# A fused retention and feed-forward kernel: the second projection of six blocks as seven products of quarters, in a new order of the work

## The chip, the core and the metric

The kernel runs on one core of a Trainium2 chip. The core has a matrix engine (TensorE, PE in the profile, with its weight loads as PEld), a vector engine (DVE), a scalar engine (ACT), a general engine (POOL, GpSimd) and a queue engine that here only issues transfers (SP). They run side by side, each through its own list of instructions in order, and wait for each other by semaphores. Data moves between HBM and on-chip memory by 16 DMA engines, which SP, ACT and POOL feed. TensorE adds its results up in eight banks of 512 f32 columns by 128 partitions; DVE and ACT read the banks, POOL cannot.

The metric is the time of one execution in microseconds on the device, lower is better.

## The reference

```python
def _attn_ref(q, k, v):                      # each (8, 8, 576, 64): batch, heads, rows, width
    scores = scale * np.matmul(q, k.transpose(0, 1, 3, 2))
    ...
    Dmat = np.where(rel >= 0, gamma[:, None, None] ** rel[None, :, :], 0.0)
    ret = scores * Dmat[None, :, :, :]
    return np.matmul(ret, v).astype(np.float32)

def _moe_ref(x, w_in, w_out, alpha):         # x: 4608 tokens of 512; w_in 512x2048, w_out 2048x512
    h = x @ w_in
    s = np.sin(alpha * h)
    g = h + s * s / (alpha + 1e-09)
    return (g @ w_out).astype(np.float32)
```

The heads' outputs of the first part, side by side, are the 512 columns of `x` in the second. Everything comes and goes as f32; the matrix engine works on f16 copies.

## The kernel before

**Blocks.** The 4608 tokens are nine blocks of 512. Blocks 0 to 7 are the first 512 rows of the eight batches; block 8 is made of the last 64 rows of all of them. For each block the kernel computes the retention and then the feed-forward part:

- LD loads q, k or v of one half of a block (256 rows of all heads, 512 KB) into one of sixteen f32 buffers; CA scales and casts it to f16. LE and CE do the same for the last 64 rows.
- k and q are turned by TensorE and a copy (TU, TK) in blocks 0 and 1, and by a transposing transfer (XP, XE) after that.
- OU, TS or EV, MA, MB, NS and ST build the states that carry the decayed past from one 128 rows to the next. SC makes the scores in a pair of banks, MK masks them out of the banks on DVE, VA, VB and SA add up values and states in a pair of banks (RL is a mark between the two), KP copies the result to `x`.
- PR is a first projection of 128 hidden units: four matmuls of 512 tokens into one bank. SI takes the sine of the bank (ACT), SQ squares it (ACT, DVE or POOL), and PD, on DVE, adds the scaled square to the bank's contents and writes `g`; only then is the bank free. There are 16 units to a block.
- G2 is a quarter of a second projection: four matmuls of 128 tokens x 512 columns, sixteen (four G2) to a bank for 128 tokens. FI copies the bank out, OS sends it to the output in two transfers.

WI and WO are the eight transfers of the weights, issued by POOL, which cast from f32 to f16 on the way. G2.n.c.p reads the rows of `w_out` that WO.p brings. KB are matmuls on zeros that fill waits of TensorE early on.

**The order** is not found at run time: it is the list `STEPS` (line 23 on). Each step has the form `kind.numbers:engine name=place`, where the engine letter is A (ACT), V (DVE), G (POOL) or P (PE); PD, MK, NS and AD are always on DVE, SI on ACT. `name=place` puts a tile into a numbered buffer or bank, and `<step` makes a step wait for another. The loop at line 896 emits the steps one by one, so every engine runs its steps in the order of the list. All waits that data, buffers and banks need are set by the framework; a step waits for them with everything behind it on its engine.

In `PR.1.7.2 hps.1.7=6`, for instance, unit 7 of block 1 goes into bank 6, with all 512 tokens (the last 2; 0 and 1 are the halves of 256). A score, value or `o` name takes two banks: `o.1.0=0` is banks 0 and 1.

Around the place where the two orders part, the kernel before does the following. SP issues its loads without a pause as buffers allow: all six of block 0, then 1.q.1, 1.q.0, 1.v.0, 1.k.0, 1.k.1, 1.v.1, 2.k.1, 2.k.0, 2.q.0, 2.v.0, 2.v.1, 3.k.1. POOL issues WI.0, WI.2, WI.1, WI.3, WO.0, WO.1, WO.2, WO.3. TensorE, at the end of block 0's first projection, runs PR.0.15, PR.0.13, G2.0.1.0, G2.0.1.1, SC.1.0.1, OU.1.0, SC.1.0.0, G2.0.3.0, G2.0.3.1, TU.1.k.1.2, G2.0.3.2, SC.1.1.1, SC.1.1.0, OU.1.1, G2.0.1.2, G2.0.0.0, the values and states of block 1, G2.0.3.3, G2.0.1.3, and then block 1's first projection. DVE runs there PD.0.13, the two halves of TK.1.k.1, MK.1.1.1, MK.1.1.0, ST.1.2, NS.1.3, and only then casts of block 2: CA.2.k.1.0, CA.2.k.1.1, CA.2.k.0.2. From block 3 on, units of one block's first projection alternate with the second projection of the block before, one PR to one G2.

The functions TT, SM, PP, CP, AD and OQ stand in the file but no step before calls them.

Of the kernel before, what the change touches and what calls it, by code (L numbers as in the profile page):

```python
# [23 lines left out]
CN; AR; EY; MC; Z0; ZE; FS; LD.0.k.0 raw.0.k.0=0; LD.0.q.0 raw.0.q.0=1; LD.0.v.0 raw.0.v.0=2; LD.0.q.1 raw.0.q.1=3  # L24
LD.0.k.1 raw.0.k.1=4; CA.0.k.0.0:G k16.0.0=0; LD.0.v.1 raw.0.v.1=5; CA.0.q.0.1:V q16.0.0=1; CA.0.k.0.1:V; CA.0.q.0.0:V
CA.0.v.0.2:A v16.0.0=2; LD.1.q.1 raw.1.q.1=6; KB.16.256.6; KB.44.64.6; OU.0.0 kv.0.0.0=0 kv.0.0.1=1
# [188 lines left out]
def kernel(  # L215
# [10 lines left out]
    nc = tc.nc  # L226
# [4 lines left out]
    P = 128  # L231
# [77 lines left out]
    def halves(n):  # L309
        return slice(64 * n, 64 * n + 64)  # L310
# [631 lines left out]
```

## Time and profile before

| | |
|---|---|
| median of three runs | 311.0 us (309.82 to 311.75) |
| profiled execution | 310.68 us |
| its span, first to last instruction | 308.9 us |
| granted TensorE clock, mean | 0.991 |
| first projection (L757), 608 matmuls | 143.1 us busy |
| second projection (L796), 576 matmuls | 142.3 us busy |
| DMA packets | 49.84 MB, 161 GB/s on average |

Line numbers are those of the listing above: L757 is PR, L765 SI, L775 and L776 SQ, L780 PD, L796 G2, L313 all copies and casts, L436 CA of q and k, L386 WO, L539 SC, L570 VA and VB, L606 SA, L552 MK, L512 MA, L515 MB, L520 NS, L526 ST. "L780 DVE ... x144 | 106.2, 746 | 54.3 <-ACT s L775 46.1" means: 144 instructions of that line on DVE were busy for 106.2 us, 746 ns each; before them DVE sat idle for 54.3 us, 46.1 of which ended with ACT's instruction of line 775. In a timeline a row has start, length, engine, line, operation, and in brackets the idle time before it with what ended it; neighbours of a kind are merged (x8). Matmuls overlap, so the length of one (379 ns for 512 columns) is more than the distance between two; distances are read from the starts. A DMA share is a mean over the 16 engines; it can exceed 1 where transfers overlap.

### The profile page before, as it was taken

The numbers are of one execution on the slowest core, as the hardware profiler recorded it, in microseconds if no ns is written. First come the engines' busy times: TensorE is split into PE (matmuls) and PEld (weight loads), VectorE is DVE, ScalarE is ACT, GpSimd is POOL, SyncE is SP. The second block draws the span as 40 slices with busy tenths as digits, with TensorE's granted clock in tenths as the row PEclk, the third lists the DMA queues.
The fourth block names the chain that finished last, engine by engine and source line by source line (L and its number), as shares of the span: only waits on it lengthen the run. The fifth ranks groups of instructions, "written<-read, shape, count | busy, mean of one in ns | idle before, by whom it ended". The sixth has DMA issues, their size and how long they took to land.

```text
span 308.9 us, 7892 instructions
## 1 busy us (share of the span) xinstructions
PE 294.2 (95%) x3241; PEld 148.1 (48%) x3241; DVE 204.6 (66%) x297; ACT 181.4 (59%) x287; POOL 136.6 (44%) x154
## 2 busy tenths in 40 slices
PE   7769999999999999999999999899999999999994
PEld 5645556455444544454445444444454454444441
DVE  1587989899778786767666566766657745556500
ACT  1538946685356667675777577556764556555411
POOL 5794680299379497487168613970030000000000
PEclk9799999999999999999999999999999999999998
DMA  7999999997893978688797979774431111111232
GB/s 230 336 216 216 219 256 317 257 245 214 214 304 97 166 172 227 189 155 176 164 262 175 152 169 235 191 174 105 102 70 36 34 36 37 34 34 43 56 73 69
DMA packets 115380, 49.84 MB, mean 161 GB/s; under 512 B 69760, under 2 KB 110736, under 8 KB 115344
## 3 DMA queue, kind: packets, MB, share of 16 engines
q1 hardware_dynamic: 110912, 45.10, 61.3%
q0 software_dynamic: 4224, 4.19, 8.0%
q8 instruction: 25, 0.41, 0.6%
q10 hardware_dynamic: 208, 0.04, 0.1%
q14 instruction: 11, 0.09, 0.1%
HBM read 36.74 MB, written 9.44 MB: 149 GB/s over the span
## 4 chain that ended last, share of the span: by engine, by line
PE 64%; DMA 9%; POOL 8%; DVE 6%; SPq 5%; issue 4%; ACT 2%; POOLq 0%; ACTq 0%; DVEq 0%
PE banks L796 30%; PE banks L757 27%; DMA r<-in_q_dram 4%; POOL h L436 4%; SPq L409 3%; DVE g L780 2%; DMA r<-in_k_dram 2%; PE banks L539 2%; PE banks L570 2%; DMA r<-in_v_dram 2%; DMA s<-s 2%; DVE h L552 1%; DVE s L776 1%; POOL s L776 1%; ACT s L765 1%
## 5 line engine op out<-in xcount | busy, mean ns | idle before, releaser
L757 PE MATMUL banks<-r,w_in 128*128 128x512 f16 (+1 forms) x608 | 143.1, 368 | 1.1 <-DVE g L780 0.9
L796 PE MATMUL banks<-w_out,g 128*128 128x512 f16 x576 | 142.3, 379 | 0.1
L780 DVE SCALAR_TENSOR_TENSOR g<-s,inva,banks 128x512 f16<-128x512 f16 x144 | 106.2, 746 | 54.3 <-ACT s L775 46.1
L765 ACT ACTIVATE s<-banks,alpha 128x512 f16<-128x512 f32 x144 | 97.1, 687 | 71.3 <-PE banks L757 67.9
L757 PEld LDWEIGHTS <-w_in 128*128 128x128 f16 x608 | 58.4, 98 | 65.4 <-issue 1.6
L796 PEld LDWEIGHTS <-g 128*128 128x128 f16 x576 | 54.8, 98 | 65.0 <-issue 0.4
L436 POOL TENSOR_TENSOR h<-r,cn 128x1024 f16<-128x1024 f32 (+1 forms) x29 | 49.7, 1723 | 36.3 <-DMA r<-in_k_dram 24.2
L776 DVE TENSOR_TENSOR s<-s 128x512 f16<-128x512 f16 x72 | 40.3, 560 | 20.4 <-ACT s L765 18.0
L313 ACT COPY h<-banks 128x512 f32<-128x512 f32 (+2 forms) x41 | 25.9, 639 | 30.3 <-PE banks L796 21.5
L775 ACT ACTIVATE s<-s 128x512 f16<-128x512 f16 x62 | 38.8, 631 | 1.1
L552 DVE TENSOR_TENSOR h<-banks,mask 128x1024 f16<-128x1024 f32 (+1 forms) x32 | 35.2, 1119 | 2.5 <-PE banks L539 2.4
L313 ACT CAST r<-banks 128x1024 f16<-128x1024 f32 (+1 forms) x18 | 15.5, 873 | 8.3 <-PE banks L606 6.2
L644 POOL TENSOR_TENSOR s<-h,cn 128x512 f16<-128x512 f32 x8 | 8.7, 1087 | 23.1 <-PE banks L570 18.2
L515 POOL TENSOR_TENSOR r<-h,r 128x256 f32<-128x256 f32 x22 | 16.2, 735 | 3.2 <-ACT r L313 1.7
L313 POOL CAST h<-r 128x1024 f16<-128x1024 f32 (+1 forms) x10 | 10.1, 1016 | 14.2 <-DMA r<-in_v_dram 14.1
L776 POOL TENSOR_TENSOR s<-s 128x512 f16<-128x512 f16 x10 | 10.3, 1037 | 12.5 <-ACT s L765 12.5
L436 DVE TENSOR_TENSOR h<-r,cn 128x512 f16<-128x512 f32 (+1 forms) x11 | 10.9, 1031 | 5.3 <-DMA r<-in_q_dram 5.3
L512 POOL TENSOR_TENSOR h<-r,cn 128x256 f32<-128x256 f32 x22 | 14.3, 650 | 0.2
L570 PE MATMUL banks<-h 64*64 64x128 f16 (+1 forms) x512 | 11.0, 214 | 2.9 <-POOLq L587 1.1
L526 POOL TENSOR_TENSOR h<-r,cn 128x256 f16<-128x256 f32 x19 | 12.8, 676 | 0.8 <-ACT r L313 0.2
L539 PE MATMUL banks<-h 64*64 64x128 f16 (+1 forms) x512 | 11.1, 218 | 0.8 <-ACT r L313 0.5
L539 PEld LDWEIGHTS <-h 64*64 64x64 f16 x512 | 7.8, 108 | 7.9 <-issue 6.7
(48 smaller groups left out, 107.3 us busy)
## 6 DMA issues: line engine op xcount, KB each, us to landing
out_dram<-h SPq DMA_DIRECT2D x72, 128.0 KB, 2.5
r<-in_q_dram SPq DMA_DIRECT2D x16, 512.0 KB, 6.0
r<-in_k_dram SPq DMA_DIRECT2D x10, 512.0 KB, 13.6
r<-in_v_dram SPq DMA_DIRECT2D x10, 512.0 KB, 6.0
r<-in_k_dram SPq DMA_DIRECT2D x24, 128.0 KB, 3.2
r<-in_v_dram SPq DMA_DIRECT2D x24, 128.0 KB, 3.3
w_in<-in_moe_w_in_dram POOLq DMA_DIRECT2D x4, 512.0 KB, 11.7
w_out<-in_moe_w_out_dram POOLq DMA_DIRECT2D x4, 512.0 KB, 11.0
```

The source lines that it names most:

```text
L313: return eng.copy(d_, s_) if eng is nc.scalar else eng.tensor_copy(d_, s_)
L436: return eng.tensor_tensor(dst[:, a0:a1].rearrange("p a r t d -> p t (a r) d"), t_.rearrange("p (t a) x -> p t a x", t=2)[:, :, a0:a1].rea ...
L515: return eng.tensor_tensor(sum_of(b, c), s32(b, c), sum_of(b, c), ADD)
L539: i = matmul(sc[halves(g), t, c : c + n], kT[halves(t), 2 * a + r, halves(g)], qT[halves(t), 2 * a : 2 * a + 2, 64 * g + i0 : 64 * g + 64] ...
L552: return nc.vector.tensor_tensor(ret(b, p, y).rearrange("p t (z x) -> p (t z) x", z=2)[:, :, 0:n], bank(f"sc.{b}.{p}.{y}", 2).rearrange("p ...
L570: made.append(matmul(o[halves(e), t, c : c + 128].rearrange("p (r i) -> p r i", r=2)[:, :, i0:64], v16[halves(g), 4 * t + 2 * x + e, r, :] ...
L757: i = matmul(bank(hps)[:, cols], w_in16[:, a, u * P : (u + 1) * P], x_of(n)[:, a, cols], start=starts(hps), stop=(a == KT - 1), skip_group ...
L765: return nc.scalar.activation(small(f"s.{name}")[:, cols], bank(f"hps.{name}")[:, cols], mybir.ActivationFunctionType.Sin, bias=0.0, scale ...
L775: return nc.scalar.activation(ss_t, s_t, mybir.ActivationFunctionType.Square)
L776: return eng.tensor_tensor(ss_t, s_t, s_t, MULT)
L780: return nc.vector.scalar_tensor_tensor(g_of(n)[:, u, cols], small(f"ss.{name}")[:, cols], inva[:, u : u + 1], bank(f"hps.{name}")[:, cols ...
L796: i = matmul(bank(f"op.{n}.{c}"), g_of(n)[:, fk, c * P : (c + 1) * P], w_out16[:, fk, :], start=starts(f"op.{n}.{c}"), stop=True, skip_gro ...
```

## The change

**Seven products.** Blocks 0 to 2 keep their second projection. In blocks 3 to 8 `g` (512 tokens x 2048) and `w_out` (2048 x 512) are each taken as 2 x 2 quarters, and the four quarters of the output (256 tokens x 256 columns) come from seven products instead of eight, with sums and differences of quarters as operands. Each product is 16 matmuls of 128 tokens x 256 columns for one bank (4 PP steps of 4 matmuls). The steps are:

```python
    def TT(t, i, eng):      # half of a difference of quarters of w_out, once, before block 3
    def SM(n, s, i, eng):   # half of a sum or difference of quarters of g, 128x1024 f16; 8 to a block
    ...
    BANK_OF = {1: "X", 6: "X", 7: "X", 4: "X", 2: "Y", 5: "Z", 3: "Z"}
    ...
    KEPT = {2: ("Y", "p2"), 6: ("X", "u2"), 7: ("X", "u3"), 4: ("X", "c21")}
    def CP(n, p, eng):      # copy of a bank after product p; 128x512 f32
        b, t = KEPT[p]
        return copy(eng, mid32(f"{t}.{n}"), bank(f"{b}.{n}"))
    SUMS = {11: ("X", "p2"), 22: ("Z", "u3"), 12: ("Z", "u2")}
    def AD(n, c, h=2):      # on DVE: a kept copy += a bank; 128x512 f32
        ...
        return nc.vector.tensor_tensor(x, bank(f"{b}.{n}")[:, cols], x, ADD)
```

So bank X holds product 1, is added to p2 (AD.11), takes product 6, is copied (CP.6), takes product 7, is copied (CP.7), takes product 4 and is copied (CP.4); Z takes product 5, is added to u3 (AD.22), takes product 3 and is added to u2 (AD.12); Y only product 2. A product can't start before the copy or the sum that reads its bank before it. OQ sends a quarter of the output in two transfers (block 8's last sum goes in halves).

| steps | before | after |
|---|---|---|
| G2 (4 matmuls of 512 columns) | 144 | 48 |
| PP (4 matmuls of 256 columns) | 0 | 168 |
| FI / CP / AD | 36 / 0 / 0 | 12 / 24 / 19 |
| SM on DVE / POOL; TT on DVE / POOL | 0 | 28 / 20; 6 / 2 |
| OS / OQ (two transfers each) | 36 / 0 | 12 / 25 |
| SQ on ACT / DVE / POOL | 62 / 72 / 10 | 77 / 35 / 32 |
| CA on ACT / DVE / POOL | 5 / 15 / 39 | 11 / 23 / 25 |
| MA, MB, ST on DVE / POOL | 6 / 70 | 33 / 43 |

EV, KP, FI, CE and RL change engines in a few places each. Nothing else of the work differs.

**The order.** Up to the middle of block 1 TensorE runs the same steps in the same order, with other fillers KB; on the other engines CA.1.q.0, CA.1.k.0, SQ.0.7, SQ.0.10 go from POOL to DVE, SQ.0.3 and SQ.0.12 from POOL to ACT, and POOL's weight transfers become WO.1 (waits for SI.0.8), WO.0, WO.3 (waits for SI.0.15), WO.2. SP's loads after 1.k.1 become 2.k.1, 1.v.1, 3.q.0, 2.q.0, 2.v.1, 3.k.1, 2.k.0. From there on the order is new. Its first part (after the first lines, which are cut):

```diff
-CA.1.q.1.2:G q16.1.1=12 <ST.0.0; KB.10.256.3; OU.0.1 kv.0.1.0=0 kv.0.1.1=1; MA.0.2:G s32.0.2=13; TS.0.2:A
...
+WO.1 <SI.0.8; SQ.0.3:A ss.0.3=8; PD.0.3; SI.0.11 s.0.11=9; PR.0.7.2 hps.0.7=3; TK.1.q.0.1:V; WO.0; SI.0.6 s.0.6=10
...
+SQ.0.9:V ss.0.9=12; PD.0.4; SI.0.15 s.0.15=11; G2.0.1.0 op.0.1=4; PD.0.9; SQ.0.15:A ss.0.15=7; WO.3 <SI.0.15; G2.0.1.1
+SQ.0.10:V ss.0.10=14; PD.0.10; SI.0.13 s.0.13=15; PD.0.15; WO.2; SC.1.0.1 sc.1.0.1=6; OU.1.0 kv.1.0.0=0 kv.1.0.1=3
+LD.2.q.0 raw.2.q.0=0; ST.0.3:V; TS.1.0:A kvs.1=1; TS.1.1:A; SC.1.0.0 sc.1.0.0=0; SQ.0.13:A ss.0.13=0
+G2.0.3.0 op.0.3=3; MA.1.1:V s32.1.1=24; MB.1.1:V; G2.0.3.1; CA.1.k.1.2:V k16.1.1=25; PD.0.13; TU.1.k.1.2 tr.1.k.1=5
+MK.1.0.0 ret.1.0.0=26; G2.0.3.2; TK.1.k.1.1:V kT.1.1=27; SC.1.1.1 sc.1.1.1=0; LD.2.v.1 raw.2.v.1=2
+LD.3.k.1 raw.3.k.1=3; LD.2.k.0 raw.2.k.0=4; CA.2.k.0.2:V k16.2.0=0; MK.1.0.1 ret.1.0.1=1; TK.1.k.1.0:V
+SC.1.1.0 sc.1.1.0=6; CA.2.k.1.0:V k16.2.1=3; MA.1.2:V s32.1.2=4; CA.1.v.1.0:A v16.1.1=5; CA.1.v.1.1:A
+OU.1.1 kv.1.1.0=2 kv.1.1.1=5; TS.1.2:V; MB.1.2:G; NS.1.3; ST.1.3:V; CA.2.k.1.1:V; MK.1.1.1 ret.1.1.1=8
+ST.1.0:V s16.1=13; VA.1.0 o.1.0=0; RL.1.0:P; SA.1.0; VB.1.0; KP.1.0.2:A x.1=5; ST.1.2:V; MK.1.1.0 ret.1.1.0=9
+ST.1.1:G; VA.1.1 o.1.1=6; RL.1.1:P; SA.1.1; VB.1.1; KP.1.1.2:A; CA.2.q.0.2:V q16.2.0=15; G2.0.3.3; FI.0.3:A osb.0.3=2
+G2.0.1.2; G2.0.0.0 op.0.0=2; PR.1.13.0 hps.1.13=5; PR.1.13.1; SI.1.13 s.1.13=3; LD.3.k.0 raw.3.k.0=6
+PR.1.6.2 hps.1.6=0; SI.1.6 s.1.6=5; G2.0.1.3; FI.0.1:V osb.0.1=12; PR.1.5.0 hps.1.5=1; PR.1.5.1; SI.1.5 s.1.5=2
+LD.3.v.1 raw.3.v.1=9; LD.2.v.0 raw.2.v.0=7; XP.2.q.0 qT.2.0=14; CA.2.v.0.2:A v16.2.0=6; G2.0.0.1; PR.1.9.2 hps.1.9=4
+SQ.1.5:A ss.1.5=8; PR.1.3.2 hps.1.3=6; SI.1.3 s.1.3=10; LD.3.q.1 raw.3.q.1=12; XP.2.k.0 kT.2.0=7; PR.1.4.0 hps.1.4=7
+PR.1.4.1; SI.1.4 s.1.4=12; SI.1.9 s.1.9=11; SQ.1.13:A ss.1.13=7; SQ.1.4:V ss.1.4=15; SQ.1.9:V ss.1.9=0
+SQ.1.6:V ss.1.6=4; CA.2.v.1.2:V v16.2.1=16; PD.1.13 gT.1=1; PD.1.5; SQ.1.3:A ss.1.3=13; PD.1.3; PR.1.7.2 hps.1.7=6
+SI.1.7 s.1.7=1; SQ.1.7:V ss.1.7=6; PD.1.7; PD.1.6; CA.3.k.1.0:V k16.3.1=18; PR.1.14.2 hps.1.14=0; G2.0.0.2; G2.0.0.3
...
-G2.8.3.0 op.8.3=1; FI.8.2:A osb.8.2=22; G2.8.3.1; OS.8.2; G2.8.3.2; G2.8.3.3; FI.8.3:A osb.8.3=6; OS.8.3
+PP.8.7.2; PP.8.5.1; CP.8.7:V u3.8=26; PP.8.5.0; PP.8.4.1; AD.8.22; PP.8.4.3; OQ.8.22; PP.8.3.0; PP.8.3.1; PP.8.3.3
+AD.8.12.0; PP.8.3.2; OQ.8.12.0; PP.8.4.0; AD.8.12.1; PP.8.4.2; OQ.8.12.1; CP.8.4:A c21.8=25; OQ.8.21
...
-        return (nc.scalar if h == 1 else eng).dma_start(x[1][:, cs], t[halves(1), cs])
+        return (nc.scalar if h < 2 else eng).dma_start(x[1][:, cs], t[halves(1), cs])
```

More of the change, by code (lines that the diff above doesn't have):

```diff
@@ L23 @@
 STEPS = """
[L24 to L26 removed]
+CN; AR; EY; MC; Z0; ZE; FS; LD.0.k.0 raw.0.k.0=0; LD.0.q.0 raw.0.q.0=1; KB.41.184.6; LD.0.v.0 raw.0.v.0=2
+LD.0.q.1 raw.0.q.1=3; LD.0.k.1 raw.0.k.1=4; CA.0.k.0.0:G k16.0.0=0; LD.0.v.1 raw.0.v.1=5; CA.0.q.0.1:V q16.0.0=1
@@ L206 @@
[L206 to L210 removed]
+TK.0.k.0.0:V kT.0.0=4; TU.0.q.0.1; TS.0.0:V kvs.0=8; KB.4.256.6; TK.0.k.0.1:A; LD.1.v.0 raw.1.v.0=9
```

357 lines of the change are left out of this document (176 added, 181 removed).

## Prediction

> **What bounds the kernel now.** I read the page's busy times first, then the stretches of time, then the chain that ended last.
>
> ```profile
> PE 294.2 (95%) x3241; PEld 148.1 (48%) x3241; DVE 204.6 (66%) x297; ACT 181.4 (59%) x287; POOL 136.6 (44%) x154
> ```
>
> ```profile
> 5.00:10.00 5.00, 2.81 (x82) 2.75 (x80) 1.90 (x3) 1.04 (x1) 1.52 (x2) 0.98 1.15 346
> 10.00:15.00 5.00, 4.61 (x68) 3.68 (x66) 3.44 (x6) 2.76 (x5) 4.91 (x6) 0.68 1.16 339
> 40.00:45.00 5.00, 4.50 (x102) 2.69 (x101) 4.19 (x6) 2.34 (x6) 4.13 (x6) 1.00 1.18 271
> 280.00:300.00 20.00, 20.00 (x95) 9.04 (x94) 7.26 (x12) 7.55 (x13) 0.00 (x0) 1.00 0.20 47
> ```
>
> The columns are stretch, length, busy time of PE, weight loads, DVE, ACT, POOL, granted clock, DMA share, GB/s. PE is full at the end and nearly full at 40 us, while the DMA share is above 1 in the first three stretches: transfers are the scarce thing early, PE late. The chain ends in the last block's second projection, and the end of the timeline shows what follows it:
>
> ```profile
> 289.78 14.69 PE banks L796 x68
> ```
>
> ```profile
> 304.49 0.58 ACT L313 COPY h<-banks 128x512 f32<-128x512 f32 x1 [2.87 <-PE banks L796]
> 305.61 0.60 SPq L807 DMA_DIRECT2D out_dram<-h  x1
> ```
>
> 68 matmuls of 512 columns take 14.69 us, 216 ns each. PE stops at 304.5; copy, issue and landing take the other 4.4 us of the 308.9 us span. The profiled execution took 310.68 us, 1.78 over its span and 0.3 under the median of 311.0.
>
> **What is saved on PE.** Blocks 3 to 8 drop 6 x 64 = 384 matmuls of 512 columns (82.9 us at 216 ns) and get 6 x 112 = 672 of 256 columns. The trace has such matmuls, each with new weights, in the split first projections: PR.0.8.0 is four of them, and the first 512-wide one follows.
>
> ```profile
> 25.14 1.03 PE L757 MATMUL banks<-r,w_in 128*128 128x256 f16 x6 [0.37 <-DVE g L780]
> 25.58 1.03 PE L757 MATMUL banks<-r,w_in 128*128 128x512 f16 x4
> ```
>
> Four starts in 0.44 us are 110 ns each. At half of 216, 108 ns, the products cost 72.6 us: **-10.4 us**; at 110 ns it would be -9.0. I take -10.4, since the 0.44 holds a start as well.
>
> **The loads, where the new order begins.** The change reorders the load queue and the weight loads. Before, LD.2.k.0 is the 14th load on SP's queue and its cast on DVE is the first of this row:
>
> ```profile
> 49.38 2.36 DVE L436 TENSOR_TENSOR h<-r,cn 128x1024 f16<-128x1024 f32 x2
> ```
>
> After, it is the 18th, and its cast CA.2.k.0.2 stands on DVE *between* TK.1.k.1.1 and MK.1.0.1, TK.1.k.1.0, which block 1's scores wait for. No buffer lets SP issue it earlier than its place in the queue. WO.2 moves as well: it was issued at 29.77, second of a pair; now it follows WO.3, which waits for SI.0.15, so about 39. G2.0.3.2, its first reader, stands in the same place on PE.
>
> ```profile
> r<-in_q_dram SPq DMA_DIRECT2D x16, 512.0 KB, 6.0
> ```
>
> ```profile
> HBM read 36.74 MB, written 9.44 MB: 149 GB/s over the span
> ```
>
> ```profile
> 28.39 0.80 POOL L386 DMA_DIRECT2D w_out<-in_moe_w_out_dram  x1
> 29.77 0.81 POOL L386 DMA_DIRECT2D w_out<-in_moe_w_out_dram  x1
> 38.35 0.80 POOL L386 DMA_DIRECT2D w_out<-in_moe_w_out_dram  x1
> 53.33 2.21 POOL L313 CAST h<-r 128x1024 f16<-128x1024 f32 x2 [7.11 <-DMA r<-in_v_dram]
> ```
>
> ```profile
> DMA to landing us min/median/max: 8.7/11.0/14.2
> ```
>
> ```profile
> 42.82 1.14 ACT L313 CAST h<-r 128x512 f16<-128x512 f32 x2 [1.56 <-DMA r<-in_v_dram]
> ```
>
> Two waits date the queue. ACT at 42.82 waited for the 12th load (LD.1.v.1), POOL at 53.33 for the 17th (LD.2.v.1). A load reads 0.524 MB; a weight chunk 1.05 MB (f32; 36.74 MB less 28.3 of q, k and v is 8.4 for eight). With seven and eight chunks that is 13.6 MB at 42.8 and 17.3 MB at 53.3: 0.35 MB per us, as in the stretch at 5 us (346). The 18th load with all eight chunks lands 1.5 us later, at 54.8. Were WO.2 and WO.3 (2.1 MB) behind it, 48.8, but then G2.0.3.2, directly ahead on PE, waits for them until 54.8 instead; WO.2's own dating is 39 + 8.7 to 14.2. So PE gets past this point at about 55 in any case.
>
> The two new waits stand on POOL: behind WO.1 (after SI.0.8, so about 28) are WO.0, WO.3 (after SI.0.15), WO.2 and then MB.1.2, which nobody misses before 55. WO.0 was issued ahead of that row pair; now, at about 29, it lands between 37.4 and 42.9 by the spread above, and its reader G2.0.1.0 was at 37.5 (first row below): up to 5 us of waiting on PE, all of it inside the wait that ends at 55, and real only if that one is gone.
>
> What PE did there before, and the durations of what follows:
>
> ```profile
> 37.51 1.89 PE L796 MATMUL banks<-w_out,g 128*128 128x512 f16 x8
> ...
> 43.04 1.03 PE L796 MATMUL banks<-w_out,g 128*128 128x512 f16 x4
> 44.00 0.64 PE L539 MATMUL banks<-h 64*64 64x128 f16 x32
> ...
> 44.83 1.90 PE L796 MATMUL banks<-w_out,g 128*128 128x512 f16 x8
> 46.66 0.64 PE L570 MATMUL banks<-h 64*64 64x128 f16 x32
> ...
> 48.38 1.90 PE L796 MATMUL banks<-w_out,g 128*128 128x512 f16 x8
> ```
>
> ```profile
> L780 DVE SCALAR_TENSOR_TENSOR g<-s,inva,banks 128x512 f16<-128x512 f16 x144 | 106.2, 746 | 54.3 <-ACT s L775 46.1 <-POOL s L776 3.9
> L765 ACT ACTIVATE s<-banks,alpha 128x512 f16<-128x512 f32 x144 | 97.1, 687 | 71.3 <-PE banks L757 67.9 <-DVE g L780 1.6 <-DVE h L552 1.1
> L776 DVE TENSOR_TENSOR s<-s 128x512 f16<-128x512 f16 x72 | 40.3, 560 | 20.4 <-ACT s L765 18.0 <-DMA s<-s 1.6
> L775 ACT ACTIVATE s<-s 128x512 f16<-128x512 f16 x62 | 38.8, 631 | 1.1
> L552 DVE TENSOR_TENSOR h<-banks,mask 128x1024 f16<-128x1024 f32 x20 | 23.8, 1219 | 2.5 <-PE banks L539 2.4
> ...
> L515 POOL TENSOR_TENSOR r<-h,r 128x256 f32<-128x256 f32 x22 | 16.2, 735 | 3.2 <-ACT r L313 1.7
> ...
> L436 DVE TENSOR_TENSOR h<-r,cn 128x1024 f16<-128x1024 f32 x3 | 3.9, 1319 | 0.0
> ...
> L313 DVE CAST h<-r 128x1024 f16<-128x1024 f32 x2 | 2.2, 1114 | 0.0
> ...
> L526 DVE TENSOR_TENSOR h<-r,cn 128x256 f16<-128x256 f32 x5 | 2.2, 452 | 1.9 <-POOL r L515 1.9
> L520 DVE SCALAR_TENSOR_TENSOR r<-r,cn,banks 128x64 f32<-128x64 f32 x8 | 1.7, 275 | 0.0
> L313 DVE COPY h<-banks 128x512 f16<-128x512 f16 x4 | 1.6, 420 | 2.1 <-PE banks L454 2.1
> ...
> L313 DVE COPY h<-banks 128x512 f32<-128x512 f32 x2 | 1.4, 680 | 0.0
> ```
>
> After the landing DVE runs CA.2.k.0.2 (1.32), MK.1.0.1 (1.22), TK.1.k.1.0 (0.42): 57.8. SC.1.1.0 starts there; before, it was the second half of the row at 44.00, so 44.2. **Wait for the load: +13.6.** Bounds: 0 if the data came in time, 13.6 as dated.
>
> Then the order on DVE makes PE follow DVE. VA.1.0 needs the banks that MK.1.1.1 reads, and ahead of that stand: TS.1.2 (after OU.1.1 at about 58.6; priced like the 0.42 copy, 59.0), MB.1.2 on POOL (0.74: 59.7), NS.1.3 (four at 0.275: 60.8), ST.1.3 (0.45), a half cast CA.2.k.1.1 (half of 1.32) and MK.1.1.1 itself (1.22): 63.2. ST.1.0, ST.1.2 and MK.1.1.0 (2.1) free the other pair at 65.3; its share of the values and states (half of 46.66 to 48.38, 0.9) ends at 66.2. There G2.0.3.3 starts; before it was 48.38, with G2.0.1.2 and G2.0.0.0 (44.83 to 46.66, 1.8) already done. 66.2 - 46.6 = 19.6: **+6.0 beyond the load** (0 if PE had other work to run here; it has 1.7 us, which the list puts later).
>
> Block 1's first projection then waits on its own banks. After PR.1.4 PE can only run PR.1.7, in PR.1.3's bank. Its release by PD.1.3 stands behind SI.1.4 and SI.1.9 (0.69 each), then on DVE SQ.1.9, SQ.1.6 (0.42 each without neighbours, below), CA.2.v.1.2 (1.11), PD.1.13, PD.1.5, PD.1.3 (0.75 each): 5.6 us. PR.1.14 needs PD.1.6, behind SI.1.7, SQ.1.7, PD.1.7: 2.6 us more. **+8.2** (0 if ACT and DVE get ahead here; before, this stretch had no wait).
>
> **What the products add.** 48 SM and 8 TT, 24 CP in place of the 24 copies FI, 19 AD; SQ changes engines often, as do CA, MA, MB, ST. On DVE: 28 SM and 6 TT of 1024 elements (0.8, near two lone squares of 0.42; bounds 0.7 and 1.4) 27 us, AD 13.6 (18 at the 746 row), CP 6, 27 state steps (452) 12, some 8 more casts 9, others 8, less 37 squares (560) 21: 204.6 becomes about 260. ACT gains 15 squares and 6 casts and loses copies, about +6; POOL gets 20 SM, 2 TT and 22 squares for 14 casts and 27 state steps less, and had 172 us free. None exceeds PE's 284, so I price them at nothing, with PE as cover; DVE at 92% of it is a thin one, and a rival. The early casts and squares moved to DVE (3.5 us) and ACT, and the longer fillers KB, hide under the load wait; uncovered they cost up to 3.5. The 25 OQ issue 50 DMAs in place of 48, on queues idle by then. At the end the products of block 8 alternate with copies that PE must await, and CP.8.4 stands on ACT behind a DMA issue (0.6 on SP): +0.7 (0 to 1.5).
>
> ```profile
> L776 DVE TENSOR_TENSOR s<-s 128x512 f16<-128x512 f16 x27 | 19.4, 718 | 8.4 <-ACT s L765 8.0
> ```
>
> ```profile
> L776 DVE TENSOR_TENSOR s<-s 128x512 f16<-128x512 f16 x21 | 8.9, 423 | 6.8 <-ACT s L765 6.8
> ```
>
> The first row is from 110 to 230 us, with POOL at work, the second from 240 to 300, with POOL idle: the same square takes 718 or 423 ns. The Trainium skill, "SBUF — State Buffer", section "Who interferes with whom", says that a DVE instruction with two SBUF inputs and a GpSimd instruction that reads SBUF exclude each other for the whole instruction. The two rows agree, and the rule speaks against a change that puts work of both kinds on both engines to the end: by it the time would be the third rival's, by the lone square's row it stays at the sum below.
>
> **Sum:** 308.9 - 10.4 + 13.6 + 6.0 + 8.2 + 0.7 = 327.0 of span, + 1.8 = **329 us**.
>
> The stretch from 10 to 15 us, after PE's idle time, ran at a clock of 0.68 and so lost 1.6 us of 5. The Trainium skill, "TensorE: Matmul & The Clock Gate", Part 1, has the clock halve after an idle window of some 3.4 us until as long a busy one; by it two or three of the waits above would add an estimated 1.7 us each, 332 to 334.
>
> **Rivals.**
> *The load is in time and PE stays the bound* (faster): 308.9 - 10.4 + 0.7 + 1.8 = 301. It decides at LD.2.k.0 landing before 44 us, and the banks of block 1 freeing in time. For it: PE at 95% pays every column saved. Against: 17.8 MB by 44 us is 0.43 MB per us, which no stretch shows. 0.17.
> *Only the load wait stays*, the DVE strings run under other work: 301 + 13.6 = 315, some 310 to 317. For it: before, PE hardly waited for DVE. 0.20.
> *DVE becomes the bound* after block 1: some 100 two-input instructions (SM, TT, SQ, state steps) at up to 0.295 more (718 less 423) are 30 us, DVE 290 against PE's 284, and it idled 11 us for the load: up to 17 more, taken at 11: 340. 0.18.
> *The forecast*, 318 to 335: 0.45.
>
> The range reaches from 305, where it takes in the worst quarter of the faster case (298 to 307), to 345: it leaves out some 0.13 below and 0.05 above. A change under 1% (308 to 314) is what a measurement of this kernel can't tell from none: 0.11, from the second rival; faster 0.17, slower 0.72.
>
> **What will show it.** DVE waiting for a load of k until about 55 us ahead of a cast on L436; PE's first scores after it near 58; the products' matmuls of 256 columns 108 ns apart; PE idle near 76 to 85 for DVE L780; DVE squares at 0.7 us into the last third. Wrong if PE is busy through 44 to 66 us, or if DVE rather than PE is full after 90 us.

## The result, and the profile after

The changed kernel takes 343.7 us (median of four runs, 342.0 to 345.8) where the kernel before took 311.3 beside it: ratio 1.103, interval 1.098 to 1.108. It is slower by 32 us. The execution profiled, the longest of the four, took 345.8 us, with a span of 343.9. One kernel below, wo2_early_casts_late, ran in two groups, two runs near 332 us and four from 336.9 to 340.7 at a lower granted clock: its ratio and its profile are of the faster two, and why the four are longer no kept trace shows.

First the busy times on the page of after, and its row of the granted clock (40 slices of 8.6 us):

```profile
PE 304.4 (89%) x3529; PEld 184.5 (54%) x3529; DVE 255.3 (74%) x367; ACT 184.0 (54%) x293; POOL 170.4 (50%) x153
...
PEclk9868997578599999999879999999999999999999
```

TensorE was 95% busy and is 89% busy now, with ten microseconds *more* of busy time although it has 82.9 - 73.4 = 9.5 us less to do (the pace of the products is read below). The clock row says why for the most part: ten slices show 8 or less, where before there were two. Stretches of after, in the columns of the prediction (stretch, length, busy PE, weight loads, DVE, ACT, POOL, clock, DMA share, GB/s):

```profile
55.00:60.00 5.00, 1.65 (x4) 0.40 (x3) 2.73 (x5) 0.00 (x0) 0.00 (x0) 0.65 0.90 212
60.00:65.00 5.00, 1.64 (x65) 1.41 (x65) 2.44 (x8) 0.00 (x0) 1.29 (x2) 0.50 0.00 0
65.00:70.00 5.00, 3.55 (x90) 2.48 (x90) 3.94 (x5) 1.31 (x2) 0.00 (x0) 0.50 0.02 5
70.00:75.00 5.00, 5.00 (x20) 2.34 (x19) 0.00 (x0) 1.30 (x2) 0.00 (x0) 0.64 0.84 182
...
80.00:85.00 5.00, 1.24 (x10) 0.87 (x9) 2.86 (x6) 2.99 (x5) 1.34 (x1) 0.88 0.34 77
85.00:90.00 5.00, 1.86 (x4) 0.55 (x4) 2.29 (x5) 0.69 (x1) 0.00 (x0) 0.50 0.63 185
```

From 55 to 65 and from 80 to 90 us no engine has much to do, and the DMA engines stand still for a while too: everything waits for everything. The four long waits of TensorE, from its timeline (start, length; in brackets the idle time before it and what ended it):

```profile
58.35 1.86 PE L809 MATMUL banks<-w_out,g 128*128 128x512 f16 x4 [5.60 <-DMA w_out<-in_moe_w_out_dram]
...
66.06 0.64 PE L583 MATMUL banks<-h 64*64 64x128 f16 x16 [4.42 <-DVE h L565]
...
85.96 1.86 PE L770 MATMUL banks<-r,w_in 128*128 128x512 f16 x4 [4.72 <-DVE g L793]
90.50 1.86 PE L770 MATMUL banks<-r,w_in 128*128 128x512 f16 x4 [2.68 <-DVE g L793]
```

(Line numbers of after are 13 higher: L770 is PR, L793 PD, L809 G2, L583 VA and VB, L565 MK, L449 CA, L789 SQ on DVE and POOL, L399 WO, L539 ST; L845 is TT, L857 SM, L876 PP, L894 AD.) They are G2.0.3.2, VA.1.0, PR.1.7 and PR.1.14. Four matmuls of 512 columns take 1.86 us in these rows instead of 1.03: the clock. By PR.1.14 TensorE is 33.6 us later than before (90.5; with the order adjusted as in the prediction, before had done the same work at 56.9). What follows, all of the products included, adds another 1.4 us to that instead of taking 9.7 away.

The products themselves run as they should, here in block 8:

```profile
324.17 0.60 PE L876 MATMUL banks<-w_out,g 128*128 128x256 f16 x4
324.61 0.60 PE L876 MATMUL banks<-r,g 128*128 128x256 f16 x4
325.04 1.91 PE L876 MATMUL banks<-w_out,g 128*128 128x256 f16 x16
326.79 1.04 PE L876 MATMUL banks<-r,g 128*128 128x256 f16 x8
```

From 324.17 to 326.79 are 24 of them: 109 ns each, so 672 take 73.4 us.

### The profile page after: what moved, and what is told of

It reads as the page before. It is cut to its first block, busy times and chain, and to the rows that moved or that the text cites. A ratio compares the mean times of both kernels' runs of the same rounds, so it can differ in the third digit from the quotient of the medians.

```text
span 343.9 us, 8514 instructions
## 1 busy us (share of the span) xinstructions
PE 304.4 (89%) x3529; PEld 184.5 (54%) x3529; DVE 255.3 (74%) x367; ACT 184.0 (54%) x293; POOL 170.4 (50%) x153
## 4 chain that ended last, share of the span: by engine, by line
PE 63%; DVE 15%; DMA 6%; POOL 4%; issue 4%; ACT 4%; SPq 3%; ACTq 0%; DVEq 0%; POOLq 0%
PE banks L770 27%; PE banks L876 20%; PE banks L809 9%; DVE g L793 5%; DVE h L565 4%; DMA w_out<-in_moe_w_out_dram 3%; ACT s L778 2%; PE banks L583 2%; DVE s L789 2%; DMA r<-in_q_dram 2%; PE banks L552 2%; PE banks L500 1%; DVE h L539 1%; SPq L422 1%; POOL h L449 1%
## 5 line engine op out<-in xcount | busy, mean ns | idle before, releaser
L770 PE MATMUL banks<-r,w_in 128*128 128x512 f16 (+1 forms) x608 | 143.9, 377 | 8.5 <-DVE g L793 8.3
L793 DVE SCALAR_TENSOR_TENSOR g<-s,inva,banks 128x512 f16<-128x512 f16 x144 | 102.4, 741 | 20.3 <-ACT s L788 14.4
L770 PEld LDWEIGHTS <-w_in 128*128 128x128 f16 x608 | 58.7, 100 | 64.5 <-issue 13.6
L809 PE MATMUL banks<-w_out,g 128*128 128x512 f16 x192 | 50.0, 402 | 5.6 <-DMA w_out<-in_moe_w_out_dram 5.6
L876 PEld LDWEIGHTS <-g 128*128 128x128 f16 x480 | 46.5, 98 | 12.8 <-issue 1.2
L789 POOL TENSOR_TENSOR s<-s 128x512 f16<-128x512 f16 x32 | 36.0, 1132 | 30.8 <-ACT s L778 28.5
L449 POOL TENSOR_TENSOR h<-r,cn 128x1024 f16<-128x1024 f32 (+1 forms) x22 | 37.2, 1699 | 25.1 <-DMA r<-in_q_dram 21.6
L876 PE MATMUL banks<-w_out,g 128*128 128x256 f16 x288 | 39.0, 275 | 0.5 <-DVE h L894 0.5
L565 DVE TENSOR_TENSOR h<-banks,mask 128x1024 f16<-128x1024 f32 (+1 forms) x32 | 35.2, 1116 | 3.9 <-PE banks L552 3.8
L809 PEld LDWEIGHTS <-g 128*128 128x128 f16 x192 | 19.0, 102 | 29.0 <-issue 10.8
L857 POOL TENSOR_TENSOR r<-g 128x1024 f16<-128x1024 f16 x10 | 21.5, 2151 | 24.7 <-DVE g L857 19.1
L789 DVE TENSOR_TENSOR s<-s 128x512 f16<-128x512 f16 x35 | 22.0, 632 | 13.6 <-ACT s L778 13.4
L876 PE MATMUL banks<-r,g 128*128 128x256 f16 x192 | 25.5, 272 | 0.0
L876 PEld LDWEIGHTS <-r 128*128 128x128 f16 x192 | 18.4, 98 | 7.3 <-POOL r L857 1.1
L449 DVE TENSOR_TENSOR h<-r,cn 128x512 f16<-128x512 f32 (+1 forms) x18 | 17.4, 974 | 5.1 <-DMA r<-in_q_dram 5.1
L583 PE MATMUL banks<-h 64*64 64x128 f16 (+1 forms) x512 | 14.4, 242 | 6.2 <-DVE h L565 6.0
L326 DVE COPY h<-banks 128x512 f32<-128x512 f32 (+1 forms) x16 | 9.9, 617 | 11.5 <-PE banks L809 8.0
```

Source lines behind the costliest of these rows:

```text
L326: return eng.copy(d_, s_) if eng is nc.scalar else eng.tensor_copy(d_, s_)
L449: return eng.tensor_tensor(dst[:, a0:a1].rearrange("p a r t d -> p t (a r) d"), t_.rearrange("p (t a) x -> p t a x", t=2)[:, :, a0:a1].rea ...
L565: return nc.vector.tensor_tensor(ret(b, p, y).rearrange("p t (z x) -> p (t z) x", z=2)[:, :, 0:n], bank(f"sc.{b}.{p}.{y}", 2).rearrange("p ...
L583: made.append(matmul(o[halves(e), t, c : c + 128].rearrange("p (r i) -> p r i", r=2)[:, :, i0:64], v16[halves(g), 4 * t + 2 * x + e, r, :] ...
L770: i = matmul(bank(hps)[:, cols], w_in16[:, a, u * P : (u + 1) * P], x_of(n)[:, a, cols], start=starts(hps), stop=(a == KT - 1), skip_group ...
L789: return eng.tensor_tensor(ss_t, s_t, s_t, MULT)
```

## The experiments

Two theories. *Order*: the time is lost in the waits of the first 91 us, which come from the order of the list; the products are worth what TensorE saves. *DVE*: the sums, differences and additions of the products cost, and the early waits only cover it. In all kernels below the whole output is computed. Where lists are joined or steps moved, buffers get other numbers if one is taken.

### Front and products apart

```diff
 front_to_mid1, front_to_end1, front_to_block3:
-steps of after ahead of the joint
+steps of before ahead of PR.1.13.0 | ahead of G2.1.0.0 | ahead of G2.3.0.0
 then what is left of after, in its order
 late_front_no_products:
+steps of after ahead of G2.1.0.1, then what is left of before, in its order
```

> The list of before up to the values and states of block 1 and G2.0.1.3 (its last step is the one ahead of PR.1.13.0), then all remaining steps of the list after, in the order, on the engines and with the products of the latter; buffers are renumbered only where one was taken. Theory 'order' (the time is lost where TensorE waits up to 91 us, each wait where the trace after shows it): the slower start (4.5 us), the wait at G2.0.3.2 (10.8 more) and the string on DVE up to G2.0.3.3 (7.7 more) are gone, the waits for PD.1.3 and PD.1.6 stay: 343.7 - 23.0 = 321 us (317 to 325). Theory 'DVE' (the products' extra work on DVE and POOL is what costs, and the early waits only hide it): DVE stays about full after 90 us and gives most of it back, 332 or more.

> The same with the list of before up to the end of block 1's first projection (ahead of G2.1.0.0). Theory 'order': all waits up to 91 us are gone: 343.7 - 33.6 = 310 us (305 to 313), and the wait of PR.1.7 and PR.1.14 for PD is gone from the trace. Theory 'DVE': 322 or more, with TensorE idle for DVE after 100 us.

> The same with the list of before up to PR.4.1, that is with everything of before until the second projection of block 3; only the products of blocks 3 to 8 and the order around them are from after. Theory 'order': 672 products at 109 ns for 384 matmuls at 216 ns save 9.5 us, the tail and the waits at the join (8 TT and 8 SM at once, some 6 us of DVE work beside two PR of TensorE) take some of it: 303 to 307 us. Theory 'DVE': the products' sums, squares and additions make DVE the limit from block 3 on: 311 to 320, no faster than before.

> The other way round: the list of after up to the end of block 1's first projection (ahead of G2.1.0.1), then the remaining steps of before in its order and on its engines; no products anywhere, all second projections as G2. Theory 'order': the loss of the front stands alone, 311.3 + 33.6 = 345 us (340 to 347), as slow as the change or slower. Theory 'DVE': less than 330, since the front's waits would be work that the later blocks then have behind them.

| run | us | against before |
|---|---|---|
| front_to_mid1 | 319.6 (317.7 to 321.1) | 1.024 (1.017 to 1.031) |
| front_to_end1 | 306.0 (305.7 to 306.9) | 0.980 (0.974 to 0.986) |
| front_to_block3 | 324.0 (322.8 to 325.5) | 1.038 (1.032 to 1.045) |
| late_front_no_products | 349.3 (348.6 to 350.2) | 1.119 (1.113 to 1.126) |

Before took 312.0 us beside them. Three of the four speak for the theory of the order: front_to_mid1 and front_to_end1 lie inside its ranges, and late_front_no_products lies 2.3 us above its range, far from the other theory's 330. With the kernels before and after they make a square: the front of before or of after, with products or without.

| | without products | with products | products bring |
|---|---|---|---|
| front of before | 312.0 | 306.0 | -6.0 |
| front of after | 349.3 | 343.7 | -5.6 |
| the front costs | +37.3 | +37.7 | |

The two effects simply add up. "With products" stands here for all that the list of after does from the end of block 1 on: its order and its moves between engines come with the products, and no run has the products alone. With the front of before the changed kernel is 2% (1.4 to 2.6) *faster* than before, and TensorE is nearly full again where the products run. The page of that run and one stretch of it:

```profile
PE 288.2 (95%) x3529; PEld 175.3 (57%) x3529; DVE 249.2 (82%) x354; ACT 180.3 (59%) x288; POOL 189.0 (62%) x171
```

```profile
160.00:180.00 20.00, 20.00 (x314) 12.98 (x311) 16.21 (x23) 12.12 (x20) 17.14 (x12) 1.00 1.03 223
```

The run joined at block 3 missed the theory of the order by 17 us, and lies above the 311 to 320 of the theory of DVE as well. Its list puts six TT and the first SM in a heap at the joint, two TT of them on POOL, and DVE and then TensorE wait for them (timeline of that run):

```profile
145.16 2.02 DVE L845 TENSOR_TENSOR r<-w_out,r 128x1024 f16<-128x1024 f16 x3 [5.47 <-POOL r L845]
...
150.30 0.61 PE L876 MATMUL banks<-w_out,g 128*128 128x256 f16 x2 [4.53 <-DVE g L793]
```

To test that, the heap was spread out:

```diff
 block3_spread: as front_to_block3, and
+PD.3.0; TT.1.0:V   PD.3.1; TT.1.1:V   PD.3.2; TT.2.0:V   PD.3.3; SM.3.3.0:V   PD.3.4; TT.2.1:V   PD.3.5; TT.4.0:V
+PD.3.6; TT.4.1:V   PD.3.7; SM.3.3.1:V   PD.3.11; SM.3.1.0:V   PD.3.12; SM.3.2.0:G
```

> As the run with everything of before until the second projection of block 3 (324 us; there DVE waited 5.5 us for two TT on POOL at the join and TensorE 4.5 and 2.2 us for DVE), but six of the eight TT are all on DVE and stand singly behind PD.3.0 to PD.3.6, and SM.3.3, SM.3.1.0 and SM.3.2.0 behind PD.3.3 to PD.3.12 as their inputs get ready. Theory 'order': the miss of that run was the heap at the join; it goes with its cold clock, about 10 to 15 us: 312 (309 to 316). Theory 'DVE': sums and differences cost wherever they stand: 320 or more.

322.7 us (320.2 to 326.9), ratio 1.033 (1.028 to 1.039): a second miss, and by the time alone the theory of DVE has it (320 or more). The waits of 4.53 and 2.2 us at the joint are gone (1.15 is left at 151.5), but TensorE loses the time again further on:

```profile
180.82 0.61 POOL L525 TENSOR_TENSOR h<-r,cn 128x256 f32<-128x256 f32 x1 [6.73 <-DMA out_dram<-h]
...
184.14 1.41 DVE L793 SCALAR_TENSOR_TENSOR g<-s,inva,banks 128x512 f16<-128x512 f16 x2 [6.33 <-POOL s L789]
...
184.94 1.86 PE L770 MATMUL banks<-r,w_in 128*128 128x512 f16 x4 [5.44 <-DVE g L793]
```

POOL waits for a buffer until an output transfer has read it, DVE waits for POOL, TensorE for DVE. In front_to_block3 POOL stood in the same wait (5.59 us, until 180.90), and the same four matmuls started at 185.03, so what was won at the joint is lost again here. In the profiles of after and of front_to_end1 no step of POOL waits for an output transfer: this is a wait of the joined lists, not of the products. But the differences cost something where they were moved to as well: TT and SM now run on DVE from 113 to 137 us, and TensorE is busy for 17.06 and 18.69 of 20 us in the stretches from 100 and from 120, where in front_to_block3 it was 19.12 and 20.00: 3.4 us less. So in the order of before, block 3 has no room on DVE for all of them; in front_to_end1 TensorE waits for none of the TT. What a list joined at block 3 would take in good order stays open, and with it what the products are worth behind more of the order of before.

### Is DVE or POOL the limit of the products?

```diff
 sums_on_dve: as front_to_end1, and all 20 SM of POOL
-SM.n.s.i:G
+SM.n.s.i:V
```

> As the run with the list of before to the end of block 1's first projection (306.0 us), with the 20 SM that POOL makes (2.15 us each, 43 us) on DVE instead. Theory 'TensorE is the bound there' (PE busy 19.6 to 20 of 20 us in most stretches): no more than the waits for POOL's SM (0.4 us) and about nothing else change: 306 (304.5 to 307.5), with DVE at 249 + 20 x 0.8 = 265 us or less. Rival 'DVE is full' (my third rival of the prediction): 310 or more. Rival 'the two engines hold each other up': DVE's squares fall from 687 ns towards 423, DVE's busy time does not grow, and the time falls below 304.

306.7 us (305.6 to 307.9), ratio 0.983 (0.979 to 0.987): no change from 306.0. The group of squares on DVE in front_to_end1, then in this run (busy, mean ns), and the busy times of this run's page:

```profile
L789 DVE TENSOR_TENSOR s<-s 128x512 f16<-128x512 f16 x34 | 23.3, 687 | 6.5 <-ACT s L778 6.3
```

```profile
L789 DVE TENSOR_TENSOR s<-s 128x512 f16<-128x512 f16 x34 | 17.4, 513 | 7.2 <-ACT s L778 7.1
```

```profile
PE 289.6 (95%) x3529; PEld 176.5 (58%) x3529; DVE 252.3 (83%) x374; ACT 180.3 (59%) x288; POOL 145.6 (48%) x151
```

Twenty SM more raise DVE's busy time by 3.1 us, from 249.2 to 252.3, since its other work gets shorter: the same 34 squares fall from 687 to 513 ns with POOL's 43 us of SM gone. This agrees with the rule of the Trainium skill ("SBUF — State Buffer", "Who interferes with whom") that a DVE instruction with two SBUF inputs and a GpSimd instruction that reads SBUF hold each other up. It decides nothing here: TensorE is the bound of these stretches, and the time stays instead of falling below 304.

### What the front is made of

```diff
 start_wait_back
-CA.1.q.1.2:G q16.1.1=13
+CA.1.q.1.2:G q16.1.1=13 <ST.0.0
 wo2_early
-WO.1 <SI.0.8; ... WO.0; ... WO.3 <SI.0.15; ... WO.2
+WO.1 <SI.0.8; ... WO.0; WO.2; ... WO.3 <SI.0.15
 wo2_early_casts_late: as wo2_early, and on DVE
-CA.2.k.0.2; MK.1.0.1; TK.1.k.1.0; CA.2.k.1.0; ... ST.1.3; CA.2.k.1.1; MK.1.1.1; ST.1.0; ST.1.2; MK.1.1.0
+MK.1.0.1; TK.1.k.1.0; ... ST.1.3; MK.1.1.1; ST.1.0; ST.1.2; MK.1.1.0; CA.2.k.0.2; CA.2.k.1.0; CA.2.k.1.1
 waits_filled
+KB.24.512.2 (G2.0.3.2)   KB.18.512.2 (VA.1.0)   KB.20.512.3 (PR.1.7)   KB.11.512.3 (PR.1.14), each ahead of the step named
```

> The changed kernel with one thing undone: CA.1.q.1.2 on POOL waits for ST.0.0 again. Trace after: ST.0.1 and ST.0.0 on DVE take 3.50 us beside this cast instead of 0.76, MK.0.0.1 starts 2.7 us later, and the first projection 4.5 us later (25.96 against 21.42). Theory 'the start adds to the rest': the two ST take under 1 us again, the first projection starts near 21.4, and the whole 4.5 us goes: 339 us (337.5 to 340.5). Rival 'the start hides under the later waits' (WO.2's landing and the loads are dated by their own queues): 343 to 344.

341.1 us (339.3 to 345.3; ratio 1.093, 1.089 to 1.097), 2.6 less than the change: between the two expectations. The first projection starts 4.1 us earlier, with the clock from 20 to 30 us at 1.00 where after has 0.50 and 0.58, but G2.0.3.2 only 2.4 us, after a longer wait for the same WO.2:

```profile
21.89 2.08 PE L770 MATMUL banks<-r,w_in 128*128 128x256 f16 x12
...
55.91 1.87 PE L809 MATMUL banks<-w_out,g 128*128 128x512 f16 x4 [7.92 <-DMA w_out<-in_moe_w_out_dram]
```

The rest was hidden under that transfer.

> The changed kernel with WO.2 issued directly behind WO.0, ahead of WO.3 and its wait for SI.0.15. Theory 'DVE is next' (my step 2, with the scores held by CA.2.k.0.2, MK.1.0.1 and TK.1.k.1.0 on DVE, which end at 57.7 in the trace after): G2.0.3.2 starts near 52.8 without waiting, SC.1.1.0 at about 58 instead of 60.6: 2.6 us, and up to 1 more as the clock stays up: 340 us (339 to 341.5). Rival 'the landing of WO.2 is the whole of this step': the full 5.6 us or more: 338 or less.

339.6 us (339.4 to 342.9; 1.092, 1.088 to 1.096), as the first theory had it. (G2.0.3.2 starts at 47.80, earlier than the 52.8 expected: this profile has the earlier start of the last section too. That is not what the run gained, since DVE's wait below covers it.) DVE and TensorE in its timeline:

```profile
54.81 1.23 DVE L449 TENSOR_TENSOR h<-r,cn 128x1024 f16<-128x1024 f32 x1 [5.40 <-DMA r<-in_k_dram]
```

```profile
57.56 0.64 PE L552 MATMUL banks<-h 64*64 64x128 f16 x16 [7.68 <-DVE h L326]
```

With WO.2 out of the way, DVE stands at CA.2.k.0.2 until LD.2.k.0 lands at 54.8, and SC.1.1.0 follows at 57.6. This is the wait that the prediction dated. In the profile of after it isn't to be seen, because there DVE itself was late:

```profile
54.11 1.22 DVE L449 TENSOR_TENSOR h<-r,cn 128x1024 f16<-128x1024 f32 x1
```

> As the run with WO.2 early, and on DVE the casts CA.2.k.0.2, CA.2.k.1.0 and CA.2.k.1.1 stand behind MK.1.1.0 instead of between the steps that block 1's scores and values wait for (my step 3). Theory 'string on DVE': each cast's 0.65 to 1.2 us leaves the path to VA.1.0, 2.5 us in all beyond the run before: 337.5 us (336 to 339), G2.0.3.3 near 64.5 instead of 69.6. Rival 'the casts are only missed later' (block 2's turned k comes late): as the run with WO.2 early, 340.

331.6 and 332.0 us (ratio 1.065, 1.061 to 1.069). VA.1.0 in wo2_early, then here:

```profile
63.04 0.64 PE L583 MATMUL banks<-h 64*64 64x128 f16 x16 [4.41 <-DVE h L565]
```

```profile
55.45 0.64 PE L583 MATMUL banks<-h 64*64 64x128 f16 x16 [3.85 <-DVE h L565]
```

It starts 7.6 us earlier, three times the 2.5 expected, since the casts leave with their wait for the load, not only with their own length. Block 2 did not miss them: against wo2_early the time falls by as much.

> The changed kernel with matmuls on zeros put into TensorE's four long waits, in banks that are free there: 24 of 512 columns ahead of G2.0.3.2, 18 ahead of VA.1.0, 20 ahead of PR.1.7, 11 ahead of PR.1.14 (5.2, 3.9, 4.3 and 2.4 us at full clock, under the waits of 5.6, 4.4, 4.7 and 2.7). Nothing else differs. Theory 'clock' (the granted clock falls to 0.5 after such a wait and the work behind it pays): the stretches from 57.9 to 74.9 and from 85.2 to 95.4 at clock 0.5 go, and with them half of the PE work in them that DVE does not hold up, about 7 us: 337 (335 to 339.5). Rival 'DVE sets the pace of these stretches': 343 to 345, the clock at 1.0 all the same.

340.8 us (336.7 to 342.3; 1.091, 1.086 to 1.096), 2.9 less than the change; the forecast was 6.7, so neither theory has it all. The clock did stay up (stretches of this run):

```profile
60.00:65.00 5.00, 4.44 (x82) 2.46 (x82) 3.08 (x8) 0.00 (x0) 1.29 (x2) 1.00 0.10 27
65.00:70.00 5.00, 4.13 (x99) 2.28 (x98) 3.30 (x5) 2.56 (x3) 0.00 (x0) 1.00 0.07 16
...
85.00:90.00 5.00, 4.70 (x23) 2.05 (x21) 3.75 (x7) 0.69 (x1) 0.00 (x0) 1.00 0.69 203
```

PR.1.14 starts at 88.14 instead of 90.50. Doing nothing useful in the four waits gains 2.9 us: that is about what the clock that falls in them costs. (From 20 to 30 us it is as low here as in after, 0.50 and 0.63.) What is left of the waits is left to DVE's pace and the transfers.

```diff
 banks_freed_first: as front_to_mid1, and
-SI.1.3; ... SQ.1.13:A; SQ.1.4:V; SQ.1.9:V; SQ.1.6:V; PD.1.13; PD.1.5; SQ.1.3:A; PD.1.3; PR.1.7; ... PD.1.7; PD.1.6
+SI.1.3; SQ.1.3:A; ... SQ.1.13:A; PD.1.3; SQ.1.4:V; SQ.1.9:V; SQ.1.6:V; PD.1.6; PD.1.13; PD.1.5; PR.1.7; ... PD.1.7
```

> As the run with the list of before up to the middle of block 1, with three steps of block 1's first projection put ahead of others (my step 4): SQ.1.3 on ACT directly behind SI.1.3, and on DVE PD.1.3 ahead of SQ.1.4 and PD.1.6 directly behind SQ.1.6, ahead of PD.1.13 and PD.1.5. Theory 'order of the releases': PR.1.7 starts near 57.8 instead of 61.3 and PR.1.14 near 59.3 instead of 65.9, and the clock no longer falls behind them (some 2.5 us more): 319.6 - 6.5 - 2.5 = 311 us (309 to 314). Rival 'ACT and DVE are short of time here, so the wait only moves to the next unit': 317 to 320.

313.8 us (311.8 to 315.7), ratio 1.006 (1.003 to 1.010), inside the first theory's range. PR.1.7 and PR.1.14 in front_to_mid1, then here:

```profile
61.31 1.87 PE L770 MATMUL banks<-r,w_in 128*128 128x512 f16 x4 [4.12 <-DVE g L793]
65.85 1.87 PE L770 MATMUL banks<-r,w_in 128*128 128x512 f16 x4 [2.67 <-DVE g L793]
```

```profile
58.79 1.02 PE L770 MATMUL banks<-r,w_in 128*128 128x512 f16 x4 [1.34 <-DVE g L793]
60.74 1.02 PE L770 MATMUL banks<-r,w_in 128*128 128x512 f16 x4 [0.93 <-DVE g L793]
```

Three steps further forward in two lists take 4.5 of 6.8 us of waiting away, and the 1.87 us rows are 1.02 again. Another 7.8 us lie between this run and front_to_end1, in the rest of block 1's order.

### A version that is faster than both

```diff
 best_of_both: as front_to_end1, and
-CP.3.7:V
+CP.3.7:A
-(nc.scalar if h < 2 else eng)
+(nc.scalar if h < 2 or (n, c) == (8, 21) else eng)
```

> As the run with the list of before to the end of block 1's first projection, with two small steps: CP.3.7 on ACT instead of DVE, where it stood behind a cast that waited for a load (TensorE waited 1.25 us for it at 152.5), and the second transfer of the last OQ issued by ACT instead of SP, where it followed the first by 0.6 us. Theory 'order': 1.2 and 0.6 us: 304.2 us (303 to 305.5), faster than before by 2.3%. Rival: both are taken up by the next waits: 306.

305.2 us (303.9 to 306.4), ratio 0.978 (0.974 to 0.983): 2.2% faster than before. It lies inside the 303 to 305.5 expected, and the wait of 1.25 us is gone from the trace; but against front_to_end1 it is 0.7 us, less than the 1.8 forecast and within what the runs scatter, so these two steps are not shown to help.

## Why the prediction was right, and where its sum was not

It forecast 329 us, slower, from three waits of the front against a saving on TensorE. The direction and the kind of cause hold; the sum was 14.7 us short. 343.7 lies outside the 318 to 335 of the forecast's own case and 1.3 us inside the range's upper bound of 345, which left room for DVE as the bound. That did not happen, so in this part the range held by luck. By its steps:

- **Saved on TensorE, -10.4.** Pace right: 109 ns for 108 forecast, -9.5. But with the tail (+0.7 forecast) the products bring only 5.6 to 6.0 net. The work at their joints was priced at nothing with PE as cover. The waits of TensorE in front_to_end1 that before didn't have (engine and line, what they were for; us in total, times, longest):

```profile
PE banks L770 <- DVE h L326: 1.3, 1, 1.3
PE banks L552 <- DMA h<-h: 0.9, 1, 0.9
PE banks L876 <- DVE h L894: 0.8, 2, 0.5
...
PE banks L876 <- POOL r L857: 0.4, 1, 0.4
```

They are 3.4 us: a copy, a transposing transfer, sums, and an SM on POOL. This term was mis-sized by some 4 us, 0.9 of it in the pace. The rows say where the rest arose but are no full account, since shorter waits of before are gone here (the longest 1.1 us).
- **Wait for the load, +13.6.** The mechanism is right and so is its date: LD.2.k.0 lands at 54.8 in wo2_early, and SC.1.1.0 starts at 57.6 (forecast 54.8 and 57.8). In after it starts near 60.6, +16.4, and the last to arrive is WO.2, which the prediction named as the other transfer that ends this wait and dated earlier. WO.2 waits for SI.0.15, and block 0 ran 9 us late: it was issued after 47.2 instead of about 39 and landed near 58.3.
- **String on DVE, +6.0.** G2.0.3.3 starts at 69.6; before, adjusted, 46.6: +23.0 for the two steps together, where 19.6 was forecast. The runs give 24.1 (343.7 - 319.6).
- **Banks of block 1, +8.2.** The two waits were forecast at 5.6 and 2.6 and measured 4.7 and 2.7. But the order of block 1 costs 13.6 us (319.6 - 306.0): the step left out that TensorE comes out of them at half clock, and the units behind, which no run takes apart.
- **Early casts, priced at nothing, as hidden under the load wait.** Wrong: this is a step that failed. The dropped wait of CA.1.q.1.2 was among the early moves, and the prediction didn't ask what that wait kept apart (last section). In the profiled run the first projection starts 4.5 us late (25.96 against 21.42), 4.1 of them for it. Undoing it gains 2.6.
- **The clock.** The prediction weighed the rule of the Trainium skill ("TensorE: Matmul & The Clock Gate", Part 1: half clock after an idle window of some 3.4 us, until as long a busy one) and left it out of the sum, with 1.7 us a wait on the side. It belonged in. The five-microsecond rows from 55 to 75 us show 0.65, 0.50, 0.50 and 0.64: 17 us at half clock and not 3.4, since the next wait comes before TensorE has been busy long enough. The trace has them from 56.49 to 73.56; cut into five pieces of 3.41 us, TensorE is busy for 1.56, 1.73, 0.64, 3.06 and 3.41 us in them, and for 0.00 in the piece before. So the clock fell behind an empty piece and came back behind the first full one, as the rule has it. With the waits filled the half clock is gone from these rows, for 2.9 us.

In sum the front costs 37.5 instead of 27.8, and the products bring 5.8 instead of 9.7; that is 13.6 of the 14.7. The rest is the base: the sum started from an execution of 310.7 us, and before took 312.0 beside the runs of the square.

**The rivals.** *PE stays the bound, 301* did not happen, yet front_to_end1 and best_of_both show how near one comes to it without the front (306 and 305). (The argument against it has a slip: 17.8 MB by 44 us is 0.40 MB per us, not 0.43, still more than the 0.35 of the stretches.) *Only the load wait*, 315: the strings ran under no other work. *DVE becomes the bound, 340*, came nearest in the number and is refuted in its mechanism: after PR.1.14 TensorE waits for DVE and POOL 5.4 us in all, from 95 us on it is busy for 238.1 of 249 us and DVE for 200.4, and in front_to_end1 20 more SM on DVE cost nothing. A number that fits is no proof of its story.

**The signs.** The pace of the products (109 ns), DVE's squares (0.70 us from 230 us on) and TensorE's idle time for PD (80 to 90 us, forecast near 76 to 85) came as named. DVE's wait for the load of k did not show in after, and the scores behind its cast came at 60.6, not near 58.

## What to carry to other kernels

Where a kernel's order is written out by hand, try a change of the work and a change of the order apart: here the later blocks, with the new work, were worth -6 us and the order of the front that came with it +37, and the two simply add. Ahead of a string of waits ask for each in-order engine which instruction stands in front of the one that others need, and where the release of a bank stands in the lists of the engines that release it. Where waits come close together, add the fallen clock to each, and don't assume that it recovers between them.

## What the runs showed that was not expected

**A wait of 2.7 us that comes and goes.** ST.0.1 and ST.0.0 on DVE and the cast on POOL, in after and then in wo2_early, where nothing before 28 us differs:

```profile
14.79 3.50 DVE L539 TENSOR_TENSOR h<-r,cn 128x256 f16<-128x256 f32 x2 [1.30 <-POOL r L528]
15.52 1.91 POOL L449 TENSOR_TENSOR h<-r,cn 128x1024 f16<-128x1024 f32 x1
```

```profile
14.68 0.76 DVE L539 TENSOR_TENSOR h<-r,cn 128x256 f16<-128x256 f32 x2 [1.30 <-POOL r L528]
...
15.42 1.92 POOL L449 TENSOR_TENSOR h<-r,cn 128x1024 f16<-128x1024 f32 x1
```

The cast starts 0.73 and 0.74 us after the pair, as the second ST ends. (0.74 in waits_filled and late_front_no_products as well.) Once DVE is held until after the cast, once not at all. It fits the exclusion above; what decides it the trace doesn't show. The wait that the kernel before had at this place makes sure of the good case; of the five profiles without it, three (after, waits_filled, late_front_no_products) have the bad one.

**Two transfers behind one wait.** WO.2 and LD.2.k.0 end within a few us of each other, each hidden by the other. Taking one away shows the second, and the gain of wo2_early (4.1 us) says little of what both cost.
